# Loading the first units' queries without the other head's zeros, and writing those zeros once with VectorE

## The chip, the core and the metric

The kernel runs on one core of one Trainium2 chip. TensorE does the matrix products, VectorE, ScalarE and GpSimd the elementwise work, and SyncE (SP) issues nearly all DMAs. The metric is the device time of one launch in microseconds (us), the median of several runs. A profiled execution gives in addition a span, which goes from its first to its last instruction.

## The reference

Chunked attention over 4 batches x 8 heads, 768 positions, head dimension 64, followed by a two-layer network over all 3072 tokens:

```python
chunk, left_ctx, right_ctx = (32, 16, 8)          # 8 memory keys ahead of each window
for c in range(nc):
    q_c = q[:, :, c_start:c_end]
    k_full = np.concatenate([mem_k, k[:, :, l_start:r_end]], axis=2)
    v_full = np.concatenate([mem_v, v[:, :, l_start:r_end]], axis=2)
    scores = scale * np.matmul(q_c, k_full.transpose(0, 1, 3, 2))
    scores = scores - np.max(scores, axis=-1, keepdims=True)
    a = np.exp(scores)
    a = a / (np.sum(a, axis=-1, keepdims=True) + 1e-09)
    out[:, :, c_start:c_end] = np.matmul(a, v_full)
x = out.transpose(0, 2, 1, 3).reshape(B * S, H * D)   # 3072 x 512
h = x @ w_in                                          # 512 -> 2048
g = np.maximum(h, 0.0) + alpha * np.minimum(h, 0.0)
return g @ w_out                                      # 2048 -> 512
```

The weights w_in and w_out are drawn as float64 and decoded on the chip.

## The kernel before

The attention is worked in units. A unit is one pair of heads (2 x 64 = 128 partitions) and a block of 384 positions, which is 12 chunks of 32. There are 32 units. The network is worked in blocks of tokens against 16 slices of the hidden width: `up` (L713) makes h with three fp32r products per k, and `down` (L742) adds g times w_out into the output banks. Each weight slice arrives by DMA as 512 KB of w_in and 512 KB of w_out (`load_w`, L593 and L594), is decoded by ScalarE and VectorE (`decode_part`, L617 to L644), and the products of that slice wait for it.

This case is about the first 8 units (`NWIN`), the start of the program. Nothing of the network can run before they have made the first tokens, and until about 35 us their work shares the engines with the decoding of the first weights. Such a unit goes through these steps:

1. `load_first` (L480): SP issues the loads from the tensor `first` into one of four buffers `early`; units 4 to 7 use the buffers of units 0 to 3 again. Columns 0 to 767 (`NQ`) of a buffer hold the queries, 768 to 1311 the keys, and 1312 to 1823 the values.
2. `score_products` (L295): first some `stir` products (L293), which multiply constants and are overwritten; `STIR` says how many. Then 12 score products (L307), each 24 halves in the records. One product takes both heads of a pair at once: its weights are 128 rows (both heads' dimensions) x 64 columns (32 queries of either head), and a head's rows are zero in the other head's columns. So the keys' 128 rows can be summed over.
3. `top`, `less`, `exps`, `total`, `inverse` (L500 to L519): the softmax, on VectorE except for the exponentials on ScalarE. `scale` (L529, L533) is on GpSimd.
4. `turn` (L541): one stir product and six transposes on TensorE, which ScalarE copies out (`keep`, L546).
5. `values` (L554): products with the unit's values, the buffer's last columns; then `split` (L469 on ScalarE, L472 on VectorE).

The order of each engine's work is fixed when the program is built. `Plan` (L120) holds steps with an engine, a planned cost, and what each reads and writes; `send` (L140) gives each engine its steps in an order that these costs decide. On the chip each engine goes through its own list in that order, and waits at a step whose inputs are not there. A changed planned cost on one engine can so change the order on the others.

In the kernel before, the zeros of the other head lie in `first` (`qd`, L922 to L924), and a unit's queries and keys come in one DMA (the first step at L489):

Of the kernel before, what the change touches and what calls it, by code (L numbers as in the profile page):

```python
# [18 lines left out]
P = 128  # L19
B, H, S, D = 4, 8, 768, 64  # L20
NM = 8
CH, LEFT, RIGHT = 32, 16, 8
# [77 lines left out]
FIRST_FRONT = 12  # L100


STIR = (8, 2, 1)

DUE_WEIGHTS, LAST_OUT = 4, 8


NWIN, NSET = 2 * NPAIR, 4

STARTS_WIN = (0, 2 * LEFT, NKT - KW)  # L110
NQ = NT * NJ * 2 * CH
# [65 lines left out]
def body(ctx: ExitStack, tc: tile.TileContext, qvw, kw, first, w_in, w_out, alpha, out):  # L177
# [37 lines left out]
        nc.gpsimd.memset(e[:, :, KW:], 1e-9)  # L215
    for ew in ews:
        nc.gpsimd.memset(ew, 0.0)
    warm = sm.tile([P, 1], F32, name="warm")
    nc.vector.memset(warm, 0.0)
    nc.scalar.activation(out=warm, in_=warm, func=AF.Exp)  # L220
# [74 lines left out]
    def score_products(u):  # L295
        blk, pr = divmod(u, NPAIR)
        st = state[u]
        s_ps = ps_s.tile([P, 512], F32, name="s_ps", tag=f"s{u % 2}")
        stir(s_ps, STIR[0] if u == 0 else STIR[1])
        st["s"] = s_ps[:, :2 * NJ * KW].rearrange("p (n k) -> p n k", k=KW)  # L300
        t = early[u % NSET]
        q = t[:, :NQ].rearrange("p (c x) -> p c x", c=NT * NJ)
        keys = t[:, NQ:NQ + NT * NKT].rearrange("p (t k) -> p t k", t=NT)
        for n in range(2 * NJ):
            for i in range(2):
                t, j = n // NJ * 2 + i, n % NJ
                nc.tensor.matmul(  # L307
                    out=st["s"][i * 2 * CH:(i + 1) * 2 * CH, n],
                    lhsT=q[:, t * NJ + j],
                    rhs=keys[:, t, STARTS_WIN[j]:STARTS_WIN[j] + KW],  # L310
                    start=True, stop=True,
                )
# [167 lines left out]
    def load_first(u):  # L480
        blk, pr = divmod(u, NPAIR)
        t = early[u % NSET]

        def load(lo, hi):
            nc.sync.dma_start(out=t[:, lo:hi], in_=first[blk, pr, :, lo:hi])  # L485

        state[u] = {}
        step(SP, 1.6, partial(load, 0, NQ + NT * NKT), writes=[("qk", u % NSET)], rest=due(u))
        step(SP, 0.78, partial(load, NQ + NT * NKT, NQ + NT * NKT + NV), writes=[("fv", u % NSET)], rest=due(u))  # L489

    def windows(u):

# [65 lines left out]
                        start=True, stop=True,  # L558
                    )

        step(PE, 1.2, partial(score_products, u), reads=[("qk", u % NSET)], writes=[sk], rest=due(u))
        step(DVE, 0.66, top, writes=[sk, ("mx", u % 3)])
        step(DVE, 0.55, less, reads=[sk, ("mx", u % 3)], writes=e_keys(u))
        step(ACT, 0.52, exps, writes=e_keys(u))
# [24 lines left out]
    def load_w(f):  # L589
        def load(i):  # L590
            k, j = ((f, i), 0) if f < NAPART else ((f, 0), i)
            if k not in raw:
                raw[k] = wps[k].tile([P, 2 if f >= NAPART else 1, DM, 2], I32, name="w_t", tag="w")  # L593
            nc.sync.dma_start(out=raw[k][:, j].rearrange("p m b -> p (m b)"), in_=srcs[i][f])  # L594

        i = f - NF + NSET
        after = [("qk", i), ("fv", i)] if i >= 0 else []
        for i in range(2):
            step(SP, 1.31, partial(load, i), writes=[("r", f, i)] + after, rest=rest(place_of(f)))

# [304 lines left out]
def _layout(q, k, v, mem_k, mem_v, moe_w_in, moe_w_out, moe_alpha):  # L905
# [13 lines left out]
    vwin = np.stack([keys(vp, mem_v, t * TQ, (-16, 16), None, (16, 104)) for t in range(S // TQ)], axis=2)  # L919
    vwin = vwin.reshape(B, NPAIR, 2, nh, NT, P, D).transpose(0, 3, 1, 5, 4, 2, 6)  # L920
    nwin = NWIN // NPAIR
    qd = np.zeros((nwin, NPAIR, 2, D, NT * NJ, 2, CH), q.dtype)  # L922
    for h in range(2):
        qd[:, :, h, :, :, h] = qT.reshape(NHALF, NPAIR, 2, D, NT * NJ, CH)[:nwin, :, h]  # L924
    kfirst = np.stack([keys(kp, mem_k, t * TQ, (-16, 16), None, (16, 104), None) for t in range(S // TQ)], axis=2)
    kfirst = kfirst.reshape(B, NPAIR, 2, nh, NT, NKT, D).transpose(0, 3, 1, 2, 6, 4, 5)
    kfirst = kfirst.reshape(NHALF, NPAIR, P, NT * NKT)[:nwin]
# [1 line left out]
    return dict(  # L929
        qvw=np.concatenate([qT.reshape(NHALF, NPAIR, P, BT), vparts], axis=3),  # L930
        kw=np.ascontiguousarray(kwin).reshape(NHALF, NPAIR, P, NT, NKT),
        first=np.concatenate([qd.reshape(nwin, NPAIR, P, NQ), kfirst, vparts[:nwin]], axis=3),
        w_in=np.ascontiguousarray(moe_w_in.reshape(NK, P, NF, P).transpose(2, 1, 0, 3)
                                  ).reshape(NF, P, NK * P).view(np.int64),
        w_out=np.ascontiguousarray(moe_w_out.reshape(NF, P, DM)).view(np.int64),
# [17 lines left out]
```

## Time and profile before

| | |
|---|---|
| median of 3 runs | 600.02 us (599.72 to 600.05) |
| the profiled execution's own time | 600.83 us |
| its span | 599.0 us |
| granted TensorE clock in it | 1.000 |
| busy: TensorE, VectorE, ScalarE, GpSimd | 592.1, 388.2, 211.1, 36.7 us |
| read from HBM, written | 41.95 MB, 6.29 MB |

The profile's page has the busy time of each engine (PE is TensorE, PEld its weight loads, DVE VectorE, ACT ScalarE, POOL GpSimd, SPq the queue of SyncE), the span in 40 slices, the chain of work that ended last, and groups of instructions by source line. The trace can be asked further: busy time in chosen stretches, waits, single DMAs and their time to landing, and instructions in order of time. In a row of the timeline stand the start, the duration, the engine, the line, the operation with its tiles, and in brackets how long the engine was idle before it and what ended that.

### The profile page before, as it was taken

The page shows a single profiled execution, that of the slowest core. Times are in us where ns is not written, and L with a number is a line of the kernel's source. Part 1 is how long each engine was busy: PE and PEld are TensorE (multiplying, and loading weights), DVE is VectorE, ACT ScalarE, POOL GpSimd, SP SyncE. Part 2 cuts the span into 40 slices and gives each one's busy share as a digit, 9 for nine tenths or more (in the row PEclk, how much of TensorE's full clock was granted, in tenths as well). Part 3 has the DMA queues.
Part 4 walks back from the last instruction along what each step waited for, and adds up shares of the span by engine and source line. Part 5 has one row for each costly group of instructions (what it writes and reads, how often), then busy time and mean ns, then how long its engine had stood idle before and what let it go on. Part 6 is the DMA issues. An engine that isn't in the chain of part 4 may idle for free.

```text
span 599.0 us, 10981 instructions
## 1 busy us (share of the span) xinstructions
PE 592.1 (99%) x4430; PEld 506.3 (85%) x4430; DVE 388.2 (65%) x904; ACT 211.1 (35%) x580; POOL 36.7 (6%) x61
## 2 busy tenths in 40 slices
PE   8999999999999999999999999999999999999997
PEld 5689898988988989899898888888888888888886
DVE  5888998887958768785885852861762771530530
ACT  3688878644222414323233301302400411210201
POOL 3410000010001101010010100100100100000000
PEclk9999999999999999999999999999999999999999
DMA  8999500222040302403204003003201000000001
GB/s 325 354 402 407 236 0 1 66 65 89 2 146 8 100 5 98 143 11 100 84 17 143 11 1 92 9 0 101 69 2 36 0 1 36 36 1 0 1 1 71
DMA packets 21076, 48.96 MB, mean 82 GB/s; under 512 B 2464, under 2 KB 5792, under 8 KB 21024
## 3 DMA queue, kind: packets, MB, share of 16 engines
q1 hardware_dynamic: 20880, 48.12, 22.7%
q8 instruction: 35, 0.57, 0.4%
q10 hardware_dynamic: 144, 0.13, 0.1%
q14 instruction: 17, 0.14, 0.1%
HBM read 41.95 MB, written 6.29 MB: 81 GB/s over the span
## 4 chain that ended last, share of the span: by engine, by line
PE 96%; DMA 2%; DVE 1%; ACT 1%; issue 0%; SPq 0%; ACTq 0%
PE h_ps L718 44%; PE o_ps L748 44%; PE a_ps L433 3%; PE s_ps L332 2%; DMA w_t<-w_in 2%; PE s_ps L293 1%; PE s_ps L307 1%; PE a_ps L554 0%; DVE w_t L629 0%; ACT qk L546 0%; PE o_ps L541 0%; ACT a L617 0%; DVE w_t L625 0%; DVE xl L472 0%; SPq L485 0%
## 5 line engine op out<-in xcount | busy, mean ns | idle before, releaser
L718 PE MATMUL h_ps<-xh,w 128*128 128x384 f32 (+1 forms) x896 | 248.8, 359 | 0.3 <-DVE w L644 0.3
L718 PEld LDWEIGHTS h_ps<-xh,w 128*128 128x128 f32 x896 | 164.8, 188 | 16.6 <-DVE w L644 0.6
L748 PE MATMUL o_ps<-w,gh 128*128 128x512 f32 x528 | 162.7, 389 | 0.0
L718 PE MATMUL h_ps<-xl,w 128*128 128x384 f32 (+1 forms) x448 | 162.6, 363 | 0.1
L727 ACT ACTIVATE g<-h_ps 128x384 f32<-128x384 f32 (+1 forms) x112 | 60.7, 542 | 194.4 <-PE h_ps L718 128.6
L730 DVE SCALAR_TENSOR_TENSOR g<-g,rise,h_ps 128x384 f32<-128x384 f32 (+1 forms) x112 | 74.8, 668 | 74.5 <-ACT g L727 73.6
L748 PEld LDWEIGHTS o_ps<-w,gh 128*128 128x128 f32 x528 | 99.1, 188 | 20.4
L408 DVE STREAM_TRANSPOSE pt<-e 32x64 f32<-32x64 f32 (+1 forms) x336 | 99.4, 301 | 7.4 <-POOL e L387 2.0
L748 PE MATMUL o_ps<-w,gl 128*128 128x512 f32 x264 | 102.8, 389 | 0.0
L718 PEld LDWEIGHTS h_ps<-xl,w 128*128 128x128 f32 x448 | 84.1, 188 | 10.2 <-DVE xl L472 0.3
L748 PE MATMUL o_ps<-w,xh 128*128 128x512 f32 x240 | 74.8, 393 | 0.0
L748 PEld LDWEIGHTS o_ps<-w,gl 128*128 128x128 f32 x264 | 49.6, 188 | 10.2
L472 DVE TENSOR_TENSOR xl<-a_ps,xh 128x384 fp32r<-128x384 f32 x32 | 17.7, 557 | 59.5 <-ACT xh L469 58.8
L748 PEld LDWEIGHTS o_ps<-w,xh 128*128 128x128 f32 x240 | 45.0, 188 | 8.9
L469 ACT CAST xh<-a_ps 128x384 fp32r<-128x384 f32 x32 | 15.0, 481 | 95.7 <-PE a_ps L433 93.7
L736 DVE CAST gh<-g 128x512 fp32r<-128x512 f32 (+1 forms) x72 | 28.8, 401 | 30.6 <-PE o_ps L748 28.2
L387 POOL TENSOR_TENSOR e<-e,den 128x384 f32<-128x384 f32 x24 | 22.7, 947 | 419.8 <-DVE den L384 270.0
L740 DVE TENSOR_TENSOR gl<-g,gh 128x512 fp32r<-128x512 f32 (+1 forms) x72 | 46.6, 648 | 1.7
L366 ACT ACTIVATE e<-s_ps,mx 128x64 f32<-128x64 f32 x144 | 43.4, 318 | 11.1 <-DVE mx L358 11.1
L748 PE MATMUL o_ps<-w,xl 128*128 128x512 f32 x120 | 46.8, 390 | 0.0
L366 ACT ACTIVATION_READ_ACCUMULATOR e<-s_ps,mx 128x1 f32 x144 | 30.4, 211 | 0.0
L805 ACT COPY o_t<-o_ps 128x512 f32<-128x512 f32 x21 | 12.2, 591 | 44.6 <-PE o_ps L748 44.1
(58 smaller groups left out, 382.6 us busy)
## 6 DMA issues: line engine op xcount, KB each, us to landing
w_t<-w_in SPq DMA_DIRECT2D x16, 512.0 KB, 10.1
w_t<-w_out SPq DMA_DIRECT2D x16, 512.0 KB, 10.0
qk<-kw SPq DMA_DIRECT2D x24, 272.0 KB, 4.4
v_t<-qvw SPq DMA_DIRECT2D x24, 256.0 KB, 2.9
out<-o_t SPq DMA_DIRECT2D x23, 256.0 KB, 2.1
early<-first SPq DMA_DIRECT2D x8, 656.0 KB, 6.3
qk<-qvw SPq DMA_DIRECT2D x24, 192.0 KB, 4.9
early<-first SPq DMA_DIRECT2D x8, 256.0 KB, 6.9
```

Source lines behind the costliest of these rows:

```text
L366: nc.scalar.activation(out=st["e"][:, i], in_=st["s"][h2][:, n], func=AF.Exp, scale=SCALE, bias=d["mx"][:, u - us[0], n, h2:h2 + 1], accum ...
L387: nc.gpsimd.tensor_tensor(out=st["e"], in0=st["e"], in1=st["den"].broadcast_to([P, NJ * 2, KW]), op=ALU.mult)
L408: nc.vector.transpose(out=pts[u % NPT][quad * CH:(quad + 1) * CH, j, t0:t0 + n1 - n0].rearrange("p t h q -> p (t h) q"), in_=(st["e"], zer ...
L433: nc.tensor.matmul(out=st["a"][h2 * D:(h2 + 1) * D, t * TQ:(t + 1) * TQ], lhsT=st["v"][:, t, h2, :], rhs=pts[u % NPT][:, :, t, h2, :], sta ...
L469: nc.scalar.copy(out=ring[k][0][:, cols], in_=st["a"][:, :BT])
L472: nc.vector.tensor_tensor(out=ring[k][1][:, cols], in0=st["a"][:, :BT], in1=ring[k][0][:, cols].bitcast(F32), op=ALU.subtract)
L718: nc.tensor.matmul(out=h["ps"][:, :n_cols], lhsT=ws[f, 0][:, wk, k * P:(k + 1) * P], rhs=parts(blk, k)[1](xk), start=(k == 0 and n == 0), ...
L727: nc.scalar.activation(out=h["g"], in_=h["ps"][:, :n_cols], func=AF.Relu, scale=-1.0)
L730: nc.vector.scalar_tensor_tensor(out=h["g"], in0=h["g"], scalar=rise[:, f:f + 1], in1=h["ps"][:, :n_cols], op0=ALU.mult, op1=ALU.add)
L736: copy(out=h["gh"], in_=h["g"])
L740: nc.vector.tensor_tensor(out=h["gl"], in0=h["g"], in1=h["gh"].bitcast(F32), op=ALU.subtract)
L748: nc.tensor.matmul(out=o_ps[tt], lhsT=h[gk][:, tt * P:(tt + 1) * P], rhs=ws[f, 1][:, wk], start=(f == first_f and i == 0), stop=(f == last ...
```

## The change

The tensor `first` no longer holds the zeros: a unit's queries take 384 columns in it and not 768. A unit's queries now come in two DMAs, one per head, each of 64 partitions x 384 columns (96 KB), into that head's own 384 columns of the buffer; the keys come in a DMA of their own (128 x 544, 272 KB); the values as before (128 x 512, 256 KB). So a unit is loaded by four DMAs in place of two, and by 192 KB less. The zeros of the other head are written by VectorE, once for each of the four buffers, in eight memsets of 64 x 384 at the start of the program, ahead of the `warm` memset. No later load touches these columns of zeros, so units 4 to 7 find them in place.

For this to be possible a head's queries have to lie together in the buffer. They were ordered by chunk, then head, then query; now by head, then query, then chunk. The 64 weight columns of a product lay side by side before; now each is 12 elements (48 bytes) from the next.

The planner's costs of the loads are other ones, and `STIR` has 7 in place of 8 products ahead of unit 0.

```diff
-STIR = (8, 2, 1)
+STIR = (7, 2, 1)
...
+    for t in early:
+        for h2 in range(2):
+            nc.vector.memset(t[(1 - h2) * D:(2 - h2) * D, h2 * BT:(h2 + 1) * BT], 0.0)
     warm = sm.tile([P, 1], F32, name="warm")
...
-        q = t[:, :NQ].rearrange("p (c x) -> p c x", c=NT * NJ)
+        q = t[:, :NQ].rearrange("p (x c) -> p c x", c=NT * NJ)
...
-        def load(lo, hi):
-            nc.sync.dma_start(out=t[:, lo:hi], in_=first[blk, pr, :, lo:hi])
+        def load(rows, to, lo, hi):
+            nc.sync.dma_start(out=t[rows, to:to + hi - lo], in_=first[blk, pr, rows, lo:hi])
...
-        step(SP, 1.6, partial(load, 0, NQ + NT * NKT), writes=[("qk", u % NSET)], rest=due(u))
-        step(SP, 0.78, partial(load, NQ + NT * NKT, NQ + NT * NKT + NV), writes=[("fv", u % NSET)], rest=due(u))
+
+        for h2 in range(2):
+            step(SP, 0.43, partial(load, slice(h2 * D, (h2 + 1) * D), h2 * BT, 0, BT), writes=[("fq", h2, u % NSET)], rest=due(u))
+        step(SP, 0.43, partial(load, slice(0, P), NQ, BT, BT + NT * NKT), writes=[("qk", u % NSET)], rest=due(u))
+        step(SP, 0.65, partial(load, slice(0, P), NQ + NT * NKT, BT + NT * NKT, BT + NT * NKT + NV), writes=[("fv", u % NSET)], rest=due(u))
...
-        step(PE, 1.2, partial(score_products, u), reads=[("qk", u % NSET)], writes=[sk], rest=due(u))
+        step(PE, 1.2, partial(score_products, u), reads=[("qk", u % NSET)] + [("fq", h2, u % NSET) for h2 in range(2)], writes=[sk], rest=due(u))
...
-        after = [("qk", i), ("fv", i)] if i >= 0 else []
+        after = [("qk", i), ("fv", i), ("fq", 0, i), ("fq", 1, i)] if i >= 0 else []
...
-    qd = np.zeros((nwin, NPAIR, 2, D, NT * NJ, 2, CH), q.dtype)
-    for h in range(2):
-        qd[:, :, h, :, :, h] = qT.reshape(NHALF, NPAIR, 2, D, NT * NJ, CH)[:nwin, :, h]
+    qfirst = qT.reshape(NHALF, NPAIR, P, NT * NJ, CH)[:nwin].swapaxes(3, 4).reshape(nwin, NPAIR, P, BT)
```

The change also moves instructions, since the planner's costs are others. SP's list from the loads of unit 4 to the first weights stands so before (`early_157` to `early_160` are the four buffers; 128x1312 is a unit's queries and keys, 128x512 its values):

```order
L485 DMA early_157<-first 128x1312
L485 DMA early_158<-first 128x1312
L485 DMA early_157<-first 128x512
L485 DMA early_159<-first 128x1312
L485 DMA early_158<-first 128x512
L594 DMA w_t_327<-w_in 128x1024
L485 DMA early_160<-first 128x1312
```

and so in the change (64x384 is one head's queries, 128x544 the keys):

```order
L489 DMA early_157<-first 64x384 x2
L489 DMA early_157<-first 128x544
L489 DMA early_157<-first 128x512
L489 DMA early_158<-first 64x384 x2
L489 DMA early_158<-first 128x544
L489 DMA early_158<-first 128x512
L489 DMA early_159<-first 64x384 x2
L489 DMA early_159<-first 128x544
L601 DMA w_t_316<-w_in 128x1024
```

The values of units 0 and 1 stand a place earlier, but the first w_in still follows the queries and keys of seven units and the values of two. Ahead of it stand 9 issues before and 23 now.

ScalarE's list in the same stretch, from the copies of unit 1's transposes (`qk_155`) to the exponentials of unit 5, stands so before (L512 is a unit's exponentials, L617 the first step of decoding the first w_in, L469 the first step of `split`):

```order
L546 COPY qk_155<-o_ps 128x384 x2
L469 CAST xh<-a_ps 128x384
L512 ACTIVATE e<-e 128x6x64
L617 ACTIVATE a<-w_t 128x512
L546 COPY qk_154<-o_ps 128x384 x2
L512 ACTIVATE e<-e 128x6x64
```

and so in the change, where L519 are the exponentials and L624 the decoding:

```order
L553 COPY qk_155<-o_ps 128x384 x2
L473 CAST xh<-a_ps 128x384
L624 ACTIVATE a<-w_t 128x512
L519 ACTIVATE e<-e 128x6x64
L553 COPY qk_154<-o_ps 128x384 x2
L473 CAST xh<-a_ps 128x384
L519 ACTIVATE e<-e 128x6x64
```

The first decoding step, which waits for the landing of w_in, stands ahead of unit 4's exponentials now, and behind them before.

More of the change, by code (lines that the diff above doesn't have):

```diff
@@ L931, in _layout @@
         kw=np.ascontiguousarray(kwin).reshape(NHALF, NPAIR, P, NT, NKT),
-        first=np.concatenate([qd.reshape(nwin, NPAIR, P, NQ), kfirst, vparts[:nwin]], axis=3),
+        first=np.concatenate([qfirst, kfirst, vparts[:nwin]], axis=3),
         w_in=np.ascontiguousarray(moe_w_in.reshape(NK, P, NF, P).transpose(2, 1, 0, 3)
```

## The prediction

> **What bounds the kernel now.** I read the page first, then busy time by stretches, then the chain of work at the start, then single loads and waits.
>
> ```profile
> PE 592.1 (99%) x4430; PEld 506.3 (85%) x4430; DVE 388.2 (65%) x904; ACT 211.1 (35%) x580; POOL 36.7 (6%) x61
> ```
>
> ```profile
> 5.05:26.60 21.55, 20.26 (x311) 14.69 (x312) 16.23 (x44) 10.46 (x24) 7.41 (x19) 1.00 0.97 360
> 26.60:36.40 9.80, 9.37 (x100) 7.34 (x99) 9.54 (x17) 8.18 (x17) 4.48 (x9) 1.00 1.01 390
> ```
>
> ```profile
> 40.00:45.00 5.00, 5.00 (x26) 4.48 (x26) 4.52 (x7) 4.96 (x8) 0.00 (x0) 1.00 1.03 410
> ```
>
> TensorE is the bound: 592.1 us of 599.0. A row of the stretches has the stretch, its length, then busy PE, PEld, DVE, ACT and POOL with counts, the granted clock, the DMA share and GB/s. From 40 us on, and in every later stretch of 5 us up to 595, TensorE has no gap. The change touches only the first 8 units, whose work ends near 36 us. So a gain or a loss has to arise before 36 us, and is then carried to the end unchanged. There TensorE has gaps of 21.55 - 20.26 = 1.29 us and 9.80 - 9.37 = 0.43 us. That is little to win from, and it bounds the gain: 1.72 us, what the interrupted products hide, and what is cut from TensorE's own list.
>
> What fills the gaps is seen in the chain of waits over the start (start, length, engine or DMA, line):
>
> ```profile
> 1.45 3.60 PE s_ps L293 x8
> 5.05 1.34 PE s_ps L307 x24
> ...
> 6.92 0.87 PE s_ps L307 x24
> ...
> 10.15 9.20 DMA w_t<-w_in
> ...
> 19.97 0.85 ACT qk L546 x2
> ...
> 35.51 0.81 PE a_ps L554 x16
> ```
>
> The longest piece is a transfer: the first w_in, issued at 10.15, landed at 19.35. ScalarE's list holds it up in order: the decoding step that waits for w_in stands ahead of unit 2's copies (19.97) and unit 5's exponentials. The transfer is late because of what is ahead of it in the queue. The loads of units 0 and 3, and that w_in (a row of the issue, then size and us to landing):
>
> ```profile
> 0.74 0.37 SPq L485 DMA_DIRECT2D early<-first  x1
> early<-first SPq DMA_DIRECT2D x1, 656.0 KB, 4.0
> 2.10 0.59 SPq L485 DMA_DIRECT2D early<-first  x1
> early<-first SPq DMA_DIRECT2D x1, 656.0 KB, 7.7
> 10.15 0.42 SPq L594 DMA_DIRECT2D w_t<-w_in  x1
> w_t<-w_in SPq DMA_DIRECT2D x1, 512.0 KB, 9.2
> ```
>
> Unit 0's load landed at 0.74 + 4.0 = 4.74, unit 3's at 2.10 + 7.7 = 9.80: three loads of 656 KB in 5.06 us, 1.69 us each or 389 KB per us, a full queue. The products with unit 1's values waited for their landing too, until 18.10, as the next rows show beside the other waits behind DMA:
>
> ```profile
> 4.98 1.27 PEld L307 LDWEIGHTS s_ps<-early 128*64 128x64 f32 x24 [0.84 <-DMA early<-first]
> 15.96 0.53 ACT L512 ACTIVATE e<-e 128x384 f32<-128x384 f32 x1
> 18.10 0.69 PEld L554 LDWEIGHTS a_ps<-qk,early 128*64 128x64 f32 x16 [0.45 <-DMA early<-first]
> 19.37 0.69 ACT L617 ACTIVATE a<-w_t 128x512 f32<-128x512 f32 x1 [2.89 <-DMA w_t<-w_in]
> 20.10 0.75 DVE L625 COPY w_t<-w_t 128x512 int16<-128x512 int16 x1 [1.66 <-ACT a L617]
> 20.70 0.54 ACT L512 ACTIVATE e<-e 128x384 f32<-128x384 f32 x1
> ```
>
> The exponentials at 15.96 are unit 4's, those at 20.70 unit 5's.
>
> **The change part by part.**
>
> *Bytes.* Each unit brings 192 KB less, 192 / 389 = 0.49 us of the queue. The first w_in stands behind the queries and keys of seven units: 7 x 0.49 = 3.5 us, so it would land near 19.35 - 3.5 = 15.9. The values of unit 1 are behind those of six: near 15.1. Both bounds of what this is worth on TensorE come from its gaps. Nothing, if other waits take their place. At most all 1.72 us, if VectorE and ScalarE keep up. One wait surely stays, that for `less` to free the score bank:
>
> ```profile
> PE s_ps L293 <- DVE e L508: 0.6, 2, 0.4
> ```
>
> ```profile
> 26.64 0.42 PE L718 MATMUL h_ps<-xl,w 128*128 128x384 f32 x1
> L718 PE MATMUL h_ps<-xh,w 128*128 128x384 f32 (+1 forms) x896 | 248.8, 359 | 0.3 <-DVE w L644 0.3
> ```
>
> That leaves 1.72 - 0.6 = 1.1 us. VectorE could follow: in 5.05 to 26.60 it was busy 16.23 of 21.55 us, and 1.66 us of its idle time is the wait for w_in itself. To the 1.1 I add 0.2 for what the gaps don't show: a product that is followed by a wait counts with its whole latency, as the single one at 26.64 does with 0.42 us, while 896 of L718 are 248.8 / 896 = 0.28 on the average. I take -1.3 us, with 0 and -2.0 as ends.
>
> *STIR.* One constant product less is 3.60 / 8 = 0.45 us on TensorE, if unit 0's data are there by then. They are 192 + 272 = 464 KB and not 656: 0.49 us less, so 4.74 - 0.49 = 4.25. But the keys are issued third, two issues of about 0.4 later, so they may land at up to 0.5 us more, 4.7. The seven products end near 4.6. Between a gain of 0.45 and none I take half, -0.2, for another reason too: the first 24 halves took 1.34 us and the next 24 only 0.87, so what starts earlier starts in the slow time, and that time may end when it did.
>
> *Memsets.* None of this form was run. The nearest rows:
>
> ```profile
> 0.91 0.48 DVE L200 MEMSET busy<- 128x512 bf16 x1 [0.91 <-PEq L944]
> 6.47 0.07 DVE L500 MEMSET s_ps<- 64x16 f32 x1 [5.07 <-PE s_ps L307]
> 30.50 0.42 POOL L578 MEMSET e<- 128x384 f32 x1
> ```
>
> 384 of 512 columns of the first are 0.36 us; GpSimd's has 0.42. Eight take 2.9 to 3.4 us, from 1.40 to 4.3 or 4.8. VectorE is idle until 6.47, so they cost 0; without this cover they would be the whole 3 us. Unit 0's scores now also wait for the first two memsets, with all of TensorE's list behind them: done by about 2.3, and the data come after 4. The `warm` memset is last, and ScalarE's first exponential behind it isn't due before VectorE's work on unit 0: 0.
>
> *SP.* 16 more issues, each 0.33 to 0.45 us when they follow each other. A unit's three are 1.3 us, within the 1.69 that its 656 KB took. To the first w_in there are 23 issues ahead: 0.74 + 23 x 0.45 = 11.1 at the earliest, against 10.15. With the 4.0 us of an unloaded landing that is 15.1, before the 15.9 above. So SP costs 0 on this path, though it has 0.8 us to spare and no more.
>
> *ScalarE's order.* Unit 4's exponentials (15.96 before) now stand behind the decoding step. With w_in at 15.9 they start at 15.9 + 0.69 = 16.6, 0.6 late. VectorE's total of unit 4 then shifts into its idle time before 20.10: 0. If w_in lands late, this costs; that is a rival below.
>
> *Weight columns 48 bytes apart.* No row has such a load. Taken as 0; its upper bound is a rival below.
>
> Sum: -1.3 - 0.2 = -1.5 us. The profiled execution has 600.83 with 599.0 of span, 1.83 around it. Its span would become 597.5, its time 599.3. It is 0.81 above the median of the runs, so against that: 600.02 - 1.5 = **598.5 us**. The likeliest case by itself goes from 597.5 (gaps all gone, 0.45 at the start) to 599.5.
>
> **Rivals.**
>
> *The queries' loads save bytes and no time; then the new order on ScalarE costs.* A load of 64 partitions reaches half of the rows of the buffer. If it moves at half the rate of one of 128, two loads of 96 KB take as long as 384 KB did. The queue is then as full as before, w_in lands near 19.35, and unit 4's exponentials wait for it: they start at 19.37 + 0.69 = 20.06 and take 0.54. VectorE's `total` of unit 4, `less` of unit 5 behind it, and the exponentials of unit 5 follow:
>
> ```profile
> L508 DVE TENSOR_TENSOR e<-s_ps,mx 128x384 f32<-128x384 f32 x8 | 4.4, 551 | 0.2
> L516 DVE TENSOR_REDUCE den<-e 128x6 f32<-128x390 f32 x8 | 4.4, 550 | 1.0 <-ACT e L512 1.0
> ```
>
> That is 20.06 + 0.54 + 0.55 + 0.55 and the hops between, about 21.8, against 20.70 in the trace. Price 1.1 us late on ScalarE and behind it TensorE, less 0.1 at the start: 601.0. It decides from a landing of w_in at 19.35 - 1.1 = 18.2 us on. For it: all loads in this trace cover 128 partitions, so nothing in it shows that the halves move at the full rate. Against it: each loads different rows, and the two follow each other at once.
>
> [...]
>
> *The spread weight columns load slower.* Rows of what is loaded now, and of the widest load with the same type:
>
> ```profile
> L307 PEld LDWEIGHTS s_ps<-early x192: 132/138/232, 5.0 to 23.8; 128*64 128x64 f32 x192
> L718 PEld LDWEIGHTS h_ps<-xh,w 128*128 128x128 f32 x15 | 2.7, 188 | 0.6 <-DVE w L644 0.6
> ```
>
> If 64 spread columns take as long as 128 close ones, a load takes 188 ns and not 138. Loads overlap (24 in 0.87 us are 36 ns each), so the pace would go to 36 x 188 / 138 = 49 ns: 24 x 13 = 0.31 us per unit, 2.5 us for eight; with no overlap 24 x 50 = 1.2 per unit. On a TensorE without gaps all of it counts: -1.5 + 2.5 = +1.0, 601.0. It decides from 1.5 / 8 = 0.19 us per unit on. For it: TensorE is the bound there. Against it: the products of 64 columns may still hide the loads, as loads of 188 ns are hidden behind every product of L718. [...]
>
> *The transfers come earlier and nothing follows.* VectorE is busy 9.54 of 9.80 us in 26.60 to 36.40 and could be the next bound, and each unit's softmax has its own chain of such steps of 0.55 us. Then only the start's 0.2 remains: 599.8. Against it are its idle 5.3 us before 26.60.
>
> **How the numbers follow.** The forecast has 0.42, the half-rate loads 0.27, the slow weight loads 0.18, no effect 0.13. A measurement of this kernel tells 0.2%, 1.2 us, from no change. The forecast gives faster in three of four cases (its range crosses 598.8), 0.32, else the same; the half-rate case slower in four of ten, 0.11, faster 0.02, else the same; the slow weight load slower in half, 0.09, with 0.01 faster; no effect is the same. Faster 0.35, same 0.45, slower 0.20. The range: down to 597.4, where all gaps and the whole product are gained; up to 601.4, which takes in both slower rivals at their price and leaves out a weight load without overlap.
>
> **What would show each step.** Landing of the first w_in: near 16 for the forecast, after 18 for the half-rate rival. Successive loads of queries and keys landing 1.2 us apart, or still 1.6 to 1.7. The 24 halves of a warm unit in 0.87 us, or over 1.1. Eight VectorE memsets of 0.36 to 0.42 us before 5 us. Products of L554 that no longer wait for `early`, and the last of them ending near 35, not at 36.32. The prediction is wrong if TensorE's gaps before 36 us are as large as before, if a warm unit's score products grow by 0.2 us, or if TensorE shows a gap after 40 us.

## The result, and the profile after

The change made the kernel slower: 607.81 us median (607.14 to 607.99) against 600.03 us for the kernel before (599.72 to 600.32), four runs of each. The ratio is 1.0123, with a 95% interval of 1.011 to 1.0136. The profiled execution has 607.14 us and a span of 605.4. The prediction of 598.5 us was on the wrong side, and its range (597.4 to 601.4) did not hold the time.

The page's row of busy times, kernel after:

```profile
PE 597.9 (99%) x4425; PEld 512.8 (85%) x4429; DVE 391.0 (65%) x912; ACT 211.2 (35%) x580; POOL 36.2 (6%) x61
```

The span grew by 605.4 - 599.0 = 6.4 us, and TensorE's busy time by 597.9 - 592.1 = 5.8 of it. So TensorE did not wait much longer: it had longer work. The row of the score products' weight loads (minimum, median and maximum in ns, then first and last start) says which. There are 24 halves a unit in the records, two for each of its 12 products. Kernel after, line L311, which was L307:

```profile
L311 PEld LDWEIGHTS s_ps<-early x192: 208/237/241, 5.2 to 29.7; 128*64 128x64 f32 x192
```

A weight load took 132/138/232 before and takes 208/237/241 now. The chain of waits over the start shows what that makes of a unit's 24 halves, and what released them, kernel after:

```profile
0.73 0.56 SPq L489
...
5.52 4.31 DMA early<-first
...
9.88 1.84 PE s_ps L311 x24
...
15.96 1.77 PE s_ps L311 x24
...
40.65 0.81 PE a_ps L561 x16
```

A warm unit's halves take 1.77 to 1.84 us where they took 0.87: 0.93 us more. The first of these rows is an issue of SP: the chain now begins with SP and runs through a load that landed at 9.83. The last values product of the early units ends at 41.46, and at 36.32 before.

TensorE's busy time by stretches, with the columns as in the prediction (stretch, length, PE, PEld, DVE, ACT, POOL, clock, DMA share, GB/s), of the kernel before:

```profile
5.05:45.00 39.95, 38.23 (x452) 29.85 (x453) 32.68 (x71) 26.86 (x51) 11.88 (x27) 1.00 0.99 379
45.00:100.00 55.00, 55.00 (x279) 50.00 (x278) 49.16 (x68) 45.17 (x58) 0.00 (x0) 1.00 0.44 175
```

and of the kernel after:

```profile
5.05:45.00 39.95, 38.84 (x423) 32.36 (x428) 27.21 (x66) 23.48 (x47) 12.17 (x27) 1.00 0.97 322
45.00:100.00 55.00, 54.26 (x272) 48.55 (x271) 50.53 (x70) 45.81 (x58) 0.00 (x0) 1.00 0.50 196
```

Before 45 us TensorE's gaps shrank, from 1.72 to 1.11 us, though the transfers came later. After 45 us there is now a gap of 0.74 us, where there was none. The loads on SP and ScalarE's first decoding step, kernel after (timeline rows, and the transfer's size and time to landing):

```profile
0.73 14.95 SPq L489 DMA_DIRECT2D early<-first  x23
15.73 0.43 SPq L601 DMA_DIRECT2D w_t<-w_in  x1
w_t<-w_in SPq DMA_DIRECT2D x1, 512.0 KB, 6.2
21.98 0.68 ACT L624 ACTIVATE a<-w_t 128x512 f32<-128x512 f32 x1 [1.93 <-DMA w_t<-w_in]
22.56 0.51 ACT L519 ACTIVATE e<-e 128x384 f32<-128x384 f32 x1
```

The 23 issues ahead of the first w_in took until 15.68, 0.65 us each on the average: 0.59 for the first 22 with the pauses between them, and 1.6 for the last one, after a wait of 0.35. So w_in was issued at 15.73 and landed at 15.73 + 6.2 = 21.9, not near 16 but 2.6 us later than before. The new memsets on VectorE, kernel after:

```profile
1.53 3.90 DVE L221 MEMSET early<- 64x384 f32 x8
```

### The profile page after: what moved, and what is told of

It is laid out like the page before. It is cut to its first block, busy times and chain, and to the rows that moved or that the text cites. A ratio compares the mean times of both kernels' runs of the same rounds, so it can differ in the third digit from the quotient of the medians.

```text
span 605.4 us, 11011 instructions
## 1 busy us (share of the span) xinstructions
PE 597.9 (99%) x4425; PEld 512.8 (85%) x4429; DVE 391.0 (65%) x912; ACT 211.2 (35%) x580; POOL 36.2 (6%) x61
## 4 chain that ended last, share of the span: by engine, by line
PE 96%; DMA 1%; SPq 1%; ACT 0%; DVE 0%; issue 0%; ACTq 0%
PE h_ps L725 44%; PE o_ps L755 43%; PE a_ps L437 3%; PE s_ps L336 2%; PE s_ps L311 2%; DMA early<-first 1%; PE a_ps L561 1%; SPq L489 1%; PE o_ps L548 1%; PE o_ps L297 0%; PE s_ps L297 0%; ACT w L648 0%; DVE g L737 0%; ACT o_t L812 0%; DVE mx L511 0%
## 5 line engine op out<-in xcount | busy, mean ns | idle before, releaser
L725 PEld LDWEIGHTS h_ps<-xh,w 128*128 128x128 f32 x896 | 164.8, 188 | 15.9
L755 PE MATMUL o_ps<-w,gh 128*128 128x512 f32 x528 | 162.7, 389 | 0.0
L755 PE MATMUL o_ps<-w,gl 128*128 128x512 f32 x264 | 102.8, 389 | 0.0
L391 POOL TENSOR_TENSOR e<-e,den 128x384 f32<-128x384 f32 x24 | 21.9, 913 | 422.2 <-DVE den L388 363.5
```

Of the source, the lines that this page charges most:

```text
L391: nc.gpsimd.tensor_tensor(out=st["e"], in0=st["e"], in1=st["den"].broadcast_to([P, NJ * 2, KW]), op=ALU.mult)
L725: nc.tensor.matmul(out=h["ps"][:, :n_cols], lhsT=ws[f, 0][:, wk, k * P:(k + 1) * P], rhs=parts(blk, k)[1](xk), start=(k == 0 and n == 0), ...
L755: nc.tensor.matmul(out=o_ps[tt], lhsT=h[gk][:, tt * P:(tt + 1) * P], rhs=ws[f, 1][:, wk], start=(f == first_f and i == 0), stop=(f == last ...
```

## The experiments

The changed kernel differs from the kernel before in the distance of the weight columns, in the planned order, in the number and shape of the loads, and in their bytes. The runs take these apart. Where a diff starts from the change, "+" is the experiment.

### Weight columns 48 bytes apart, nothing else (e2_spread)

The zeros still come from memory, in one load with the queries and keys.

```diff
-        q = t[:, :NQ].rearrange("p (c x) -> p c x", c=NT * NJ)
+        q = t[:, :NQ].rearrange("p (x c) -> p c x", c=NT * NJ)
...
-        first=np.concatenate([qd.reshape(nwin, NPAIR, P, NQ), kfirst, vparts[:nwin]], axis=3),
+        first=np.concatenate([np.ascontiguousarray(qd.transpose(0, 1, 2, 3, 5, 6, 4)).reshape(nwin, NPAIR, P, NQ), kfirst, vparts[:nwin]], axis=3),
```

> The kernel before with one thing of the change: the queries and their zeros are still loaded together in one load, but ordered so that the 64 weight columns of a score product are 48 bytes apart. Theory W (the spread weight columns cost the time): the 24 halves of a warm unit take about 1.8 us in place of 0.87, as in the profile of the change, and nearly all of 8 x 0.93 = 7.4 us is added: 605 to 608 us. Theory L (the loads cost it: 64 partitions, more issues, the new order): no effect, 599.5 to 600.5 us, and 0.9 us for the 24 halves.

Measured: 605.77 us (605.61 to 605.92), ratio 1.0091 (1.0074 to 1.0108). Its score products' weight loads, its stretches up to and after 45 us, and its first decoding step:

```profile
L307 PEld LDWEIGHTS s_ps<-early x192: 207/237/241, 5.0 to 29.4; 128*64 128x64 f32 x192
5.05:45.00 39.95, 39.01 (x424) 32.24 (x429) 27.66 (x64) 22.13 (x45) 12.24 (x27) 1.00 0.88 324
45.00:100.00 55.00, 55.00 (x279) 50.08 (x278) 49.31 (x69) 45.84 (x60) 0.00 (x0) 1.00 0.54 215
20.08 0.72 ACT L617 ACTIVATE a<-w_t 128x512 f32<-128x512 f32 x1
```

The weight loads are those of the change (237 ns). This alone makes three quarters of the loss, 5.5 of 7.4 us by the ratios. The halves are longer by more than that, 8 x 0.93 = 7.4 us, and TensorE's gaps before 45 us shrink meanwhile from 1.72 to 0.94 us. The last row has no bracket: ScalarE no longer waits for w_in, since it now comes to that step only at 20.08, when w_in has landed (18.8). On this slowed TensorE the waits for transfers cost less.

### How far apart they may stand (e2_s2, e2_s3, e2_s4)

The same edit with the queries of only 2, 3 or 4 chunks interleaved, so the columns of a product are 8, 12 or 16 bytes apart; the tensor `first` is ordered to match. For 2:

```diff
-        q = t[:, :NQ].rearrange("p (c x) -> p c x", c=NT * NJ)
+        q = t[:, :NQ].rearrange("p (g x c) -> p g c x", g=NT * NJ // 2, c=2)
...
-                    lhsT=q[:, t * NJ + j],
+                    lhsT=q[:, (t * NJ + j) // 2, (t * NJ + j) % 2],
...
```

> As the kernel before, with the weight columns 8 bytes apart, two to a line of 16 bytes. If the cost comes with each new line and two per line are enough, the 24 halves take 0.87 us as before and the time is that of the kernel before. If any column that is not next to the last one costs, 1.8 us.

> As the kernel before, with the weight columns 16 bytes apart. If the cost comes with each new line of 16 bytes, the 24 halves take about as long as with 48 bytes, 1.8 us. If any distance over one element costs by its size, they take less than that, and if only long distances cost, 0.87 us.

> The kernel before, with the weight columns of a score product 12 bytes apart (three chunks interleaved) and not side by side. 24 halves took 0.87 us at 4 and at 8 bytes, 1.58 to 1.66 at 16, 1.77 to 1.84 at 48. Theory (what counts is how many 16-byte lines the 64 columns touch: 16, 32, 64 and 64 of them, and 64 take 1.6 us, thus 25 ns for each of the 24 x 64 / 24 ... that is 1.04 ns a line and half; up to about 32 lines this hides behind the products): at 12 bytes 48 lines are touched, 48 x 1.04 = 50 ns a half, 1.2 us for 24, +2.6 for eight units, 602 or a little less. Rival (a limit: up to two columns' distance is free, anything wider is charged per column): 1.6 us for 24, 604 as at 16 bytes. Rival 2 (12 bytes is still free, since a line then still serves more than one column): 0.87 us, 600.6.

Measured, in single runs: 600.63, 602.06 and 603.95 us for 8, 12 and 16 bytes. The weight loads and a piece of the chain with a warm unit's halves, at 8 bytes:

```profile
L307 PEld LDWEIGHTS s_ps<-early x192: 135/138/229, 5.0 to 23.3; 128*64 128x64 f32 x192
13.09 0.87 PE s_ps L307 x24
```

at 12 bytes (the chain counts 22 pieces; all 24 halves are in the record):

```profile
L307 PEld LDWEIGHTS s_ps<-early x192: 164/177/223, 5.0 to 25.1; 128*64 128x64 f32 x192
8.55 1.28 PE s_ps L307 x22
```

and at 16 bytes:

```profile
L307 PEld LDWEIGHTS s_ps<-early x192: 192/217/218, 4.7 to 27.7; 128*64 128x64 f32 x192
6.93 1.58 PE s_ps L307 x24
```

| distance, bytes | 24 halves, us | ns a half |
|---|---|---|
| 4 (before) | 0.87 | 36 |
| 8 | 0.87 to 0.94 | 36 to 39 |
| 12 | 1.21 to 1.29 | 50 to 54 |
| 16 | 1.58 to 1.66 | 66 to 69 |
| 48 | 1.77 to 1.84 | 74 to 77 |

12 bytes fall between, where the expectation put them (1.2 us), and both other answers on record for it (free, or as dear as 16 bytes) fail. At 8 bytes nothing is lost beyond 0.07 us. At 12 and 16 bytes a half takes 4.1 to 4.5 ns for each byte of the distance. The starts of the halves show it without the end of the last one: they are 30, 31, 45, 60 and 67 ns apart at 4, 8, 12, 16 and 48 bytes, which is 3.75 ns a byte at 12 bytes and at 16. Beyond, the distance counts for little: 48 bytes, three times the distance of 16, take 1.8 us and not 1.6. That the cost comes by lines of 16 bytes, as the expectations put it, was an assumption, and no run shows the lines themselves. Its count for 12 bytes came true, but up to 16 bytes the lines grow as the distance does, so these runs can't part the two; and the count, the same at 16 and at 48 bytes, leaves the step from 1.6 to 1.8 us open.

### The change's order of work, nothing else (e6_order)

The planner gets the change's costs and steps, but one DMA brings queries, keys and zeros as before, side by side, with eight stir products and no memsets.

```diff
-            step(SP, 0.43, partial(load, slice(h2 * D, (h2 + 1) * D), h2 * BT, 0, BT), writes=[("fq", h2, u % NSET)], rest=due(u))
-        step(SP, 0.43, partial(load, slice(0, P), NQ, BT, BT + NT * NKT), writes=[("qk", u % NSET)], rest=due(u))
+            step(SP, 0.43, lambda: None, writes=[("fq", h2, u % NSET)], rest=due(u))
+        step(SP, 0.43, partial(load, slice(0, P), 0, 0, NQ + NT * NKT), writes=[("qk", u % NSET)], rest=due(u))
...
```

> The change's order alone: the planner's steps and costs of the change decide the order on every engine, but a unit's queries and keys with their zeros come in one load of 656 KB as before, with the layout and the 8 stirring products of before. The first w_in then lands near 19 to 20 us and unit 4's exponentials wait for it. If that costs what the second case of the prediction said, about 1 us: 600.8 to 601.5. If the order is what makes the loads dear, 603 and more.

Measured: 601.75 us (601.47 to 602.08), ratio 1.0023 (1.0014 to 1.0033), 1.4 us by the ratio, near what was expected of the order. Its loads, its first decoding step and its stretches:

```profile
0.74 8.70 SPq L486 DMA_DIRECT2D early<-first  x9
18.64 0.68 ACT L621 ACTIVATE a<-w_t 128x512 f32<-128x512 f32 x1 [2.77 <-DMA w_t<-w_in]
5.05:45.00 39.95, 38.09 (x454) 30.12 (x455) 32.02 (x72) 26.88 (x51) 12.17 (x27) 1.00 1.03 405
45.00:100.00 55.00, 54.29 (x273) 48.63 (x272) 50.20 (x68) 45.78 (x59) 0.00 (x0) 1.00 0.40 156
```

Half of it is the gap after 45 us, 55.00 - 54.29 = 0.71 us. It is the order's, since nothing else is changed here. Where the other half lies, the rows don't show: up to 45 us TensorE has only 38.23 - 38.09 = 0.14 us less than in the profiled execution of the kernel before, which was itself 0.8 us slower than the median. The trace of the change names the wait after 45 us, kernel after:

```profile
57.75 0.50 PE L755 MATMUL o_ps<-w,xl 128*128 128x512 f32 x1 [0.42 <-DVE xl L747]
```

This is a product of the network, 16 us after the last early unit, that waits for VectorE; one at 60.39 waits 0.33 us more. The trace of e6_order has two such waits too, 0.7 us together.

### The loads, one property at a time (e7_three, e5_128, e3_loads)

All three keep the order of the change and have close columns. e7_three adds to e6_order only the number of loads: the queries with their zeros come in two DMAs of 128 x 384, the keys in one. e5_128 and e3_loads leave out the zeros; e3_loads has the change's two loads of 64 x 384, e5_128 two of 128 x 192, the same bytes over all partitions. Against e6_order, e7_three has:

```diff
-            step(SP, 0.43, lambda: None, writes=[("fq", h2, u % NSET)], rest=due(u))
-        step(SP, 0.43, partial(load, slice(0, P), 0, 0, NQ + NT * NKT), writes=[("qk", u % NSET)], rest=due(u))
+            step(SP, 0.43, partial(load, slice(0, P), h2 * BT, h2 * BT, (h2 + 1) * BT), writes=[("fq", h2, u % NSET)], rest=due(u))
+        step(SP, 0.43, partial(load, slice(0, P), NQ, NQ, NQ + NT * NKT), writes=[("qk", u % NSET)], rest=due(u))
```

Against the change, e3_loads has the first of these edits, and e5_128 both; its memsets go to the columns that its loads leave out:

```diff
-        q = t[:, :NQ].rearrange("p (x c) -> p c x", c=NT * NJ)
+        q = t[:, :NQ].rearrange("p (c x) -> p c x", c=NT * NJ)
...
-            step(SP, 0.43, partial(load, slice(h2 * D, (h2 + 1) * D), h2 * BT, 0, BT), writes=[("fq", h2, u % NSET)], rest=due(u))
+            step(SP, 0.43, partial(load, slice(0, P), h2 * BT, h2 * BT // 2, (h2 + 1) * BT // 2), writes=[("fq", h2, u % NSET)], rest=due(u))
...
```

> As the run of the order alone, but a unit's queries come in two loads of 128 x 384 columns with their zeros, and the keys in one: the number of issues of the change, the bytes of before, all over 128 partitions. Theory I: SP needs 0.55 to 0.6 us for each issue as in the change, w_in is issued near 15 us, and the time is 603 to 605. Theory H: issues cost 0.4 to 0.45 us and the time is near that of the order alone, within 1 us.

> As the run of the change's loads with close weight columns, but each unit's queries come as two loads of 128 partitions x 192 columns in place of two of 64 x 384: as many issues and bytes, over all rows of the buffer (the queries are wrong ones again). Theory H (a load over half of the partitions moves at half the rate): the loads of units 1 to 3 land some 0.5 us apart sooner each, the first w_in near 16 to 17 us, and the time falls from 604.6 to 599 to 600.5. Theory I (the number of issues on SP costs it): SP is as slow, w_in is issued at 15 us again, 603.5 to 605.

> The change with one thing taken back: the score products take 64 columns that lie side by side, out of the buffers that are loaded and zeroed as in the change. The queries that a product then sees are wrong ones, so the output of the first units is wrong; loads, memsets, number of products and order are those of the change. Theory W: 0.87 us for a unit's 24 halves and a time near the one before, 599 to 601.5 us. Theory L: little is won back, 605 to 608 us.

Measured: e7_three 604.04 us (603.46 to 604.14), ratio 1.006 (1.0045 to 1.0075); e5_128 601.67 us (601.04 to 602.6), ratio 1.0023 (1.0013 to 1.0032); e3_loads 604.64 us (603.98 to 604.7), ratio 1.0069 (1.0054 to 1.0084). The 23 issues, the start of the first decoding step, the stretch up to 45 us, and the one from 2 to 20 us in which the loads run. That last one for e6_order, to compare:

```profile
2.00:20.00 18.00, 17.29 (x241) 10.89 (x240) 9.38 (x27) 5.86 (x15) 5.21 (x14) 1.00 1.00 393
```

e7_three, with SP's waits for the landing of loads in its first 14.1 us (in total, times, longest):

```profile
0.74 12.92 SPq L486 DMA_DIRECT2D early<-first  x23
21.12 0.70 ACT L621 ACTIVATE a<-w_t 128x512 f32<-128x512 f32 x1 [3.45 <-DMA w_t<-w_in]
5.05:45.00 39.95, 35.67 (x443) 28.05 (x444) 29.55 (x69) 25.28 (x49) 12.16 (x27) 1.00 1.02 381
2.00:20.00 18.00, 15.63 (x213) 9.72 (x213) 9.14 (x26) 4.50 (x11) 5.21 (x14) 1.00 1.00 351
SPq L486 <- DMA early<-first: 2.7, 7, 0.8
SPq L598 <- DMA early<-first: 0.4, 1, 0.4
```

e5_128, with its first issue ahead:

```profile
0.74 0.37 SPq L489 DMA_DIRECT2D early<-first  x1
0.74 11.33 SPq L489 DMA_DIRECT2D early<-first  x23
18.25 0.68 ACT L624 ACTIVATE a<-w_t 128x512 f32<-128x512 f32 x1 [1.81 <-DMA w_t<-w_in]
5.05:45.00 39.95, 37.67 (x455) 29.80 (x451) 32.31 (x72) 27.34 (x51) 12.18 (x27) 1.00 1.01 372
2.00:20.00 18.00, 16.03 (x230) 10.09 (x230) 10.83 (x35) 6.25 (x16) 5.21 (x14) 1.00 0.98 311
```

and e3_loads:

```profile
0.73 14.51 SPq L489 DMA_DIRECT2D early<-first  x23
21.74 0.66 ACT L624 ACTIVATE a<-w_t 128x512 f32<-128x512 f32 x1 [3.89 <-DMA w_t<-w_in]
5.05:45.00 39.95, 34.18 (x435) 27.30 (x440) 29.39 (x69) 24.89 (x50) 12.15 (x27) 1.00 1.00 341
2.00:20.00 18.00, 14.28 (x204) 9.21 (x206) 11.80 (x34) 4.51 (x11) 5.21 (x14) 1.00 0.91 259
```

- 14 more loads at full bytes cost 604.04 - 601.75 = 2.3 us: SP has issued everything ahead of w_in at 13.7 and not at 9.4, ScalarE starts decoding 2.5 us later, and TensorE loses 38.09 - 35.67 = 2.4 us. The time is the one that theory I of e7_three gave, but not for its reason, the price of an issue. An issue takes 0.33 to 0.44 us here, 8.7 us for all 23. From the ninth on an issue names the semaphore that the one eight before it used, and many wait for that load to land: the 12th is issued at 6.22, when the 4th has landed at 6.21, and w_in at 14.03, when the 16th has landed at 14.01. And the loads land late, though the DMA engines are full in both runs (1.00): cut into smaller pieces, the same bytes move at 351 GB/s and not 393.
- The same number of loads without the zeros gives this back: e5_128 stands where e6_order does, between the two expectations on record for it (600.5 and 603.5).
- The same bytes over 64 partitions cost 604.64 - 601.67 = 3.0 us. From 2 to 20 us the DMA engines are busy 0.91 of the time and not 0.98, and they move 259 GB/s and not 311, which is less for each busy us too. SP needs 14.51 us and not 11.33 for as many issues; the issues themselves take 12.9 and 9.1 of that. So the shape counts twice, in the transfer and in the issue. The time of e3_loads, too, lies between its two expectations (601.5 and 605): close columns win a part back, and not all.

The stretch from 2 to 20 us, in which keys, values and weights over 128 partitions move too, loses a sixth of its rate (259 and not 311 GB/s), and does not isolate the queries' share.

### The bytes, nothing else (e4_bytes)

Order and number of loads as before; 464 KB in place of 656 in each.

```diff
         def load(lo, hi):
+            lo = max(lo, NQ - BT)
             nc.sync.dma_start(out=t[:, lo:hi], in_=first[blk, pr, :, lo:hi])
...
+    for t in early:
+        nc.vector.memset(t[:, :NQ - BT], 0.0)
```

> The kernel before with the saved bytes alone: its list and order are unchanged, a unit's queries and keys are one load over 128 partitions of 464 KB in place of 656 (the queries' 384 columns as they are, which puts wrong ones into the products; VectorE zeroes the rest once, four memsets of 128 x 384). If the bytes are worth what the prediction said, the first w_in lands near 16 us and the time falls by 1 to 2 us, to 598.0 to 599.0. If other waits take the place of the transfer's, 599.6 to 600.2.

Measured: 599.64 us (598.91 to 600.42, 10 runs), ratio 0.999 (0.9981 to 0.9999). Its first decoding step, its stretch up to 45 us, and two pieces of its chain:

```profile
16.71 0.67 ACT L620 ACTIVATE a<-w_t 128x512 f32<-128x512 f32 x1 [0.65 <-DMA w_t<-w_in]
5.05:45.00 39.95, 39.21 (x463) 31.18 (x464) 33.15 (x73) 27.71 (x53) 12.28 (x27) 1.00 0.95 347
21.49 0.33 SPq L488
...
21.87 5.34 DMA w_t<-w_in
```

Here the prediction's first step happens nearly as written: w_in lands 2.7 us earlier, at 16.7, and TensorE's gaps before 45 us fall from 1.72 to 0.74 us. By the medians 0.6 us are won, with an interval of 0.06 to 1.1: the landing is that of the first expectation, and the time that of the second. What comes late next is the second w_in: it stands on SP's queue behind a load at 21.49 that waits for its buffer, and lands at 27.2.

### Columns and order together (e8_both)

e6_order with the queries 48 bytes apart, thus the change without its loads, its memsets and its missing stir product.

```diff
-        q = t[:, :NQ].rearrange("p (c x) -> p c x", c=NT * NJ)
+        q = t[:, :NQ].rearrange("p (x c) -> p c x", c=NT * NJ)
...
```

> The kernel before, with the change's order of work and with weight columns 48 bytes apart, but each unit's queries and keys still come in one load with the zeros. Of the changed kernel's three parts it lacks the loads alone. Alone, the columns gave 605.8 (+5.6), the order 601.8 (+1.6). Theory (a TensorE kept busy by slow weight loads hides waits): before 45 us TensorE is full as in the run of the columns alone (39.01 of 39.95 us in 5.05 to 45), so the order's wait for the first w_in is hidden and only its gap of 0.7 us after 45 us is added: 606.5. Rival (the costs add up): 600.2 + 5.6 + 1.6 = 607.4, with a gap of TensorE of about 1 us before 27 us. What then is missing to the change's 607.8 belongs to the loads: 1.3 us by the theory, 0.4 by the rival.

Measured: 606.85 us (606.83 to 607.14) against 600.42, ratio 1.0109 (1.0095 to 1.0122). Its stretches:

```profile
5.05:45.00 39.95, 39.01 (x424) 32.48 (x429) 27.06 (x65) 23.59 (x46) 12.14 (x27) 1.00 0.94 348
45.00:100.00 55.00, 54.30 (x272) 48.62 (x272) 50.54 (x69) 45.82 (x58) 0.00 (x0) 1.00 0.50 197
```

Before 45 us TensorE is as full as with the columns alone (39.01 in both), and only the gap of 0.70 us after 45 us is new. That is the picture of the theory that waits are hidden. The time lies between the two expectations (606.5 and 607.4) and its interval takes in both, so the rows decide here and not the time. The change's own loads, with the memsets, then add 1.0123 - 1.0109 = 0.0014, 0.8 us, which the intervals of the two ratios don't tell from nothing, where they cost 2.8 us on a TensorE with close columns (e3_loads against e6_order, by the ratios).

### A repaired version (e9_copy, e9_even)

Six of eight units load 464 KB in one DMA over 128 partitions, and ScalarE copies each head's queries to their places, side by side, two copies of 64 x 384 a unit. Three of the four buffers grow by 640 bytes.

```diff
+            nc.scalar.copy(out=q, in_=raw_q)
...
-        step(SP, 1.6, partial(load, 0, NQ + NT * NKT), writes=[("qk", u % NSET)], rest=due(u))
+            step(SP, 1.2, partial(load, NQ, NQ, k + BT), writes=[("qk", u % NSET)], rest=due(u))
+            for h2 in range(2):
+                step(ACT, 0.45, partial(place, h2), writes=[("qk", u % NSET)], rest=due(u))
...
```

> The kernel before, repaired in the way the runs point to, with the reference's result: six of the eight units (all but 0 and 4) load their queries without zeros and in one DMA of 464 KB with the keys, over 128 partitions; VectorE writes zeros once into three buffers (three memsets of 128 x 768); ScalarE then copies each head's 384 queries to their places side by side, two copies a unit. So neither the spread columns nor loads of 64 partitions nor 16 more issues. Theory: the first w_in, behind five such loads, lands 5 x 0.49 = 2.5 us earlier, near 16.9; the run with 464 KB for all units gained 0.6 us by the median, so 0.4 are left here: 599.8. Rival: 12 copies of about 0.45 us on ScalarE (21 us of it are about half busy at that time) stand ahead of exponentials of other units and delay them; then TensorE's gaps before 36 us grow by about 1 us: 601.2.

Measured: 604.93 us (604.36 to 605.93), ratio 1.0077 (1.0064 to 1.0091), worse than either expectation. Most of the loss did not come from the start. The group of down products, e9_copy:

```profile
L763 PE MATMUL o_ps<-w,gh 128*128 128x512 f32 x528 | 165.4, 394 | 0.0
```

Before, these 528 take 162.7 us, 389 ns each, and 264 sisters with `gl` grew in the same way (102.8 to 104.3 us): 4.2 us in all, from 149 us to the end. Most of their weights lie in buffers behind the three that grew, 1920 bytes further than before. The second version adds one unused tile, so that they lie 2048 bytes further:

```diff
+    gap = ctx.enter_context(tc.tile_pool(name="gap", bufs=1))
+    gap.tile([P, 32], F32, name="gap", tag="gap")
     dec = ctx.enter_context(tc.tile_pool(name="dec", bufs=1))
```

> The kernel e9_copy with one unused tile of 128 bytes a partition ahead of the buffers that hold the split activations `gh` and `gl`. In e9_copy three early buffers grew by 640 bytes each, and these later buffers moved by 1920 bytes; the 792 products L748 of the kernel before that load their weights from there took 394 to 395 ns and not 389, 4.2 us in all, everywhere from 300 to 595 us. With the tile they move by 2048 bytes; nothing else is changed. Theory (the move by 1920 bytes made these products slower, and the repair of the loads is by itself worth a little): 389 ns again, and 604.93 - 4.2 = 600.7; by the spans, 602.7 - 4.2 = 598.5 against 599.0 before, 599.5. Rival (the longer products come from the new order of work on VectorE or ScalarE, and the copies on ScalarE cost what they seem to): 394 ns and 604.9 as before.

Measured: 601.26 us (600.46 to 601.92, 11 runs) against 600.38, ratio 1.0014 (1.0005 to 1.0023). The same group, a copy on ScalarE and a stretch, e9_even:

```profile
L765 PE MATMUL o_ps<-w,gh 128*128 128x512 f32 x528 | 163.1, 390 | 0.0
16.77 0.51 ACT L496 COPY early<-early 64x384 f32<-64x384 f32 x1 [1.41 <-DMA early<-first]
5.05:26.60 21.55, 19.24 (x308) 14.64 (x312) 16.23 (x44) 16.49 (x36) 7.78 (x19) 1.00 1.00 358
```

The products are back at 390 ns, and the order of work is the same in both runs: the move by 1920 bytes had cost 3.7 us. The time is above both figures of the theory (600.7 and 599.5). What is left is 0.9 us slower than before: ScalarE is now busy 16.49 of 21.55 us where it was 10.46, and its list stops at a copy that waits for its load until 16.77, with the exponentials of another unit behind it. So neither of these two versions beats the kernel before; other ways of placing the queries were not run. By e4_bytes, a way that costs nothing would win about 0.6 us in the order of before.

## Why the prediction was wrong

**The step that failed most: "Weight columns 48 bytes apart", taken as 0.** Columns this far apart are not free: they measured 0.93 us per warm unit. The rival that priced it had the mechanism, but sized it by the widest load in the trace: 188 ns. The load took 237 ns, and the pace of the halves went from 36 to 75 ns, more than in proportion to the load (36 x 237 / 138 = 62). So 8 units cost 5.5 us (e2_spread) and not 2.5. The chance of 0.18 was low: the one argument against the rival, that products hide such loads on L718, rests on products of 0.28 us each, and a half here has 36 ns. The bound "with no overlap 24 x 50 = 1.2 per unit" stood in the text, held the measured 0.93, and was left out of the range; taken in, 8 x 1.2 - 1.5 = 8.1 would have put its upper end near 608. That it held is luck: with the measured load of 237 ns the same bound is 24 x 99 = 2.4 per unit.

**"SP": "0.45" each and "0.8 us to spare".** The issues took 0.65 us each on the average, 0.59 without the last one. The price came from loads of 128 partitions; a load of 64 x 384 costs SP 0.56 us at the very start, when nothing is queued, where 128 x 192 cost 0.37 (e5_128). The keys' issue behind them, 128 x 544 in both runs, took 0.58 and 0.42. With that, w_in was issued at 15.73 and not by 11.1, and even with the prediction's 4.0 us of an unloaded landing it would have come at 19.7, no earlier than before (19.35). The step also left out that smaller loads move more slowly (351 against 393 GB/s, e7_three and e6_order), and loads of 64 partitions more slowly still (259 against 311).

**"Bytes", -1.3.** The landing near 15.9 was nearly right for the bytes by themselves (16.7 in e4_bytes), and in the change it did not happen. (That unit 1's values would land near 15.1 was a slip without a consequence: in the change they stand ahead of unit 6's loads, so more than six times 192 KB are saved ahead of them.) The gain of 1.3 was mis-sized: 0.6 us, with a second wait behind the first, as the rival of no effect had it in part.

**The half-rate rival, 601.0.** Its direction was right and its size was not. The halves are slower (e3_loads against e5_128), and the new order costs 1.4 us (e6_order) against the 1.1 taken. It assumed that w_in would still land at 19.35. With the issues it landed at 21.7 in e3_loads, and loads and order came to 4.1 us by the ratio of 1.0069. That a load of 64 partitions moves at half the rate, no run shows by itself: from 2 to 20 us all loads together moved 259 and not 311 GB/s (e3_loads, e5_128).

**"So a gain or a loss has to arise before 36 us".** It does not: with the changed order TensorE has a new gap of 0.7 us after 45 us, in e6_order as in the change, half of the order's price. The order moves work of the network too, and not only the first units.

**"ScalarE's order", 0.** Unit 4's exponentials started at 22.56 and not at 16.6, since the decoding step ahead of them waited for the late w_in. In the change the rows show little cost of it, since TensorE's gaps before 45 us are smaller than before (1.11 against 1.72 us); its share of the 1.4 us on close columns (e6_order) stays open.

**"STIR", -0.2.** Unit 0's scores start at 5.2 and not at 5.05, in spite of the missing product: its third load was issued at 1.98 and, with 3.1 us to landing, came at 5.08. The start came 0.15 us later, not 0.2 earlier.

**"Memsets", 0.** Right in what it rests on: 8 of them end at 5.4, before VectorE has anything else to do. Each takes 0.38 us, as priced; with the pauses between them their pace is 0.49 us.

**How it adds up.** From the kernel before: columns +5.5, order +1.1 beside them (e8_both), the loads with the memsets +0.8 beside both, together 7.4 by the ratio. The 1.1 and the 0.8 are differences of ratios whose intervals overlap, so their sizes are rough; for the order, the gap of 0.70 us in e8_both stands beside it. One by one they would be 5.5, 1.4 and 2.8 (e3_loads less e6_order), 9.7. The fuller stretch before 45 us in e8_both (39.01 us, against 38.09 in e6_order) says that a TensorE kept busy hides the difference. In the two profiled executions, the score products grew by 14.7 - 7.8 = 6.9 us of TensorE's busy time, as the rows of this line have it:

```profile
L311 PE MATMUL s_ps<-early 128*64 128x64 f32 x192 | 14.7, 302 | 1.0 <-DMA early<-first 0.7
```

```profile
L307 PE MATMUL s_ps<-early 128*64 128x64 f32 x192 | 7.8, 235 | 0.0
```

That is more than the 6.4 us of the spans: the stir products have 1.4 us less in the records, where one is gone by the edit and four are missing.

## What to carry to other kernels

When an edit changes the layout of an operand, price the layout on the engine that is the bound before pricing the transfer that it saves: here 0.6 us of bytes stood against 5.5 us of weight loads. Price a DMA by its shape, in the issue (here 0.56 against 0.37 us) and in the transfer (259 against 311 GB/s), and where several small costs meet on one path, run the parts together and apart: here a TensorE kept busy hid part of them, and the order and the loads came to about 1.9 us beside the spread columns where they came to 4.1 with close ones. A cost with no row in the trace needs its full upper bound in the range, when nothing in the trace excludes it.

## What the runs showed of the hardware

- Weights of 64 fp32 columns load as fast with 8 bytes from one column to the next as with 4 (138 ns). At 12, 16 and 48 bytes a load takes 177, 217 and 237 ns, and 24 halves take 1.25, 1.6 and 1.8 us in place of 0.87. At 12 and 16 bytes that is 4.1 to 4.5 ns a half for each byte of the distance, at 48 bytes 1.5 to 1.6.
- SP's issue of a load depends on its shape: 0.56 us for 64 x 384, 0.37 to 0.42 us for 128 x 192, of the same 96 KB, at the start of the change and of e5_128.
- The same bytes in 23 loads and not 9 move at 351 and not 393 GB/s from 2 to 20 us, with the DMA engines full in both (e7_three, e6_order).
- Moving the buffer of the stationary operand by 1920 bytes made 792 products 5 to 6 ns longer on the average, and by 2048 bytes hardly (389, 394 to 395, 390 ns). Two distances do not give the rule.
